# Moving the high and low parts of six early weight conversions from ScalarE and VectorE to GpSimd

## The chip, the cores and the metric

One core of a Trainium2 chip runs the whole program. The metric is the device time of one execution in microseconds (us); several executions of each kernel are timed, and their median is compared. Engines are named as in the profile: PE is TensorE's matrix multiply, PEld its weight loads, ACT is ScalarE, DVE is VectorE, POOL is GpSimd and SP is SyncE, which here only issues DMAs.

## What is computed

The reference chains three blocks in float32: sliding-window attention with a distance bias, a gated block, and a second gated block with one more product inside.

```python
scores = scale * np.matmul(q, k.transpose(0, 1, 3, 2))      # q, k, v: 4 x 8 x 576 x 64
scores = np.where(mask, scores + bias[None], -1000000000.0) # window of 128 keys
attn = softmax(scores); attn_out = np.matmul(attn, v)
x = attn_out.transpose(0, 2, 1, 3).reshape(2304, 512)
x = (x @ w_a) * (x @ w_b) @ w_out                           # d_ff 1536
x = ((x @ w1) * (x @ w2) @ w3) @ w_out2                     # d_ff 1024
```

The weights reach the kernel as 64-bit floats. Each is brought on the core to a float32 value and then divided into a high part (rounded to the type that TensorE multiplies) and a low part, the rest. A product of two such numbers is three matmuls: high by low, low by high, high by high.

## The kernel before

**Stages.** The attention runs in 48 steps: four batches, three runs of query blocks in each (`RUNS`, line 36), four head pairs in each run. A step's scores (line 341, PE) are given their bias and row extremum on DVE (line 368), the exponential on ACT (line 374), and are transposed back (line 406, PE), copied out of PSUM (`pt`, line 273 on ACT or line 275 on DVE) and multiplied with v (line 428, PE). In the first two runs of batch 0 the division by the row sum comes last: PE makes a matrix of reciprocals (line 434), ACT copies it (`r`, line 450), DVE multiplies (`y`, line 452), and POOL makes the high part `x_hi` (line 458) and the low part `x_lo` (line 78, called from line 459). `r` and `y` have one buffer each: the next `y` is written only when POOL has read the last one.

**Filler.** The first gated block's matmuls for group 0 (line 593, `g1`) are put between the steps of the attention as filler. The first tile of 256 tokens is batch 0's first run: it reads `x_hi` and `x_lo` of all four head pairs, its low weights first, then `x_lo` with high weights, then the high parts. Its product is copied by ACT (`a`, line 600), multiplied on DVE (`g`, line 602), and parted into `gh` (ACT, line 605) and `gl` (POOL, line 78).

**The six conversions.** Group 0 has two chunks of weights with three matrices each, six pieces of 128x512, converted beside batch 0's steps. One conversion (`convert`, line 103) is a chain over two engines: ACT takes the absolute value (`ca`, line 113) and the exponent's marker (`ce`, line 116); DVE clamps, shifts and merges (lines 120, 123, 127, 132), all on `ca`; then `split` (line 140) writes the high part `whA` and the low part `wlA`. `ca` has three buffers and `ce` has one. Conversions are named below by the order in which they are made: the first two are the two factors of chunk 0, the third and fourth those of chunk 1, the fifth and sixth the two output matrices. Each engine works its own queue in order; PE's order is written out by hand during the attention (line 819), while that of ACT, DVE and POOL is set at build time by a scheduler, from the times that it expects.

Of the kernel before, what the change touches and what calls it, by code (L numbers as in the profile page):

```python
# [15 lines left out]
ACTF = mybir.ActivationFunctionType  # L16
# [28 lines left out]
def attention_moe_moe(ctx, tc, q, k, v, w_a, w_b, w_o, w_1, w_2, w_3, w_o2, out):  # L45
    nc = tc.nc
# [27 lines left out]
    def f32(ap):  # L74
        return ap.bitcast(F32)

    def sub(eng, out, a, b):
        eng.tensor_tensor(out=out, in0=a, in1=b, op=ALU.subtract)  # L78
# [3 lines left out]
    pools = {}  # L82
# [20 lines left out]
    def convert(raw, hi=None, lo=None, use=()):  # L103
# [32 lines left out]
        if hi is None:  # L136
            return [s0, s1, s3] + [lambda f=f: f(a) for f in use]
        return [s0, s1, s3, lambda: split(a, hi, lo)]

    def split(f, hi, lo):  # L140
        nc.scalar.activation(hi, f, ACTF.Copy)
        sub(nc.vector, lo, f, f32(hi))

    class Stages:

# [93 lines left out]
    raws, v_t = {}, {}  # L239
# [31 lines left out]
    def evict(eng, out, in_):  # L271
        if eng is nc.scalar:
            eng.activation(out, in_, ACTF.Copy)
        else:
            eng.tensor_copy(out=out, in_=in_)

    def prep(run, n):
        b, (x, i) = blocks_of(run)[0], items(run)[n]
        m = rows(i)
        hold = []  # L280

        def trans():
            ps = ps_t.tile([P, W], F32, name="tr")[:, 0:NP * m].rearrange("p (h c) -> p h c", h=NP)
            hold.append(ps)
            t = raws.pop((b, x, i))
            for hp in range(NP):
                nc.tensor.transpose(ps[:, hp, :], t[0:m, hp * P:(hp + 1) * P], ident[0:m, 0:m])  # L287

        def parted():
            ps = hold[0]  # L290
            if x == 0 and m == LAST:
                dst = [(slice(j * D, (j + 1) * D), q_t2, slice(j * D, (j + 1) * D)) for j in range(2)]
            else:
                dst = [(slice(0, P), k_t if x else q_t, slice(i * P, i * P + m))]
            if run < WHOLE:
                nc.scalar.activation(w_t[x][:, :, i * P:(i + 1) * P], ps, ACTF.Copy)
                if x == 0 or i < NB - 2:
                    return
            if b == 0:
                for o, _, c in dst:  # L300
                    d = last_t[x][o, :, (i - NB + 2) * P:][:, :, :m] if x else last_t[x][o, :, c]
                    nc.scalar.activation(d, ps[o], ACTF.Copy)
                return
            for o, (hi, lo), c in dst:
                nc.scalar.activation(hi[o, :, c], ps[o], ACTF.Copy)
                sub(nc.vector, lo[o, :, c], ps[o], f32(hi[o, :, c]))

        return trans, parted
# [216 lines left out]
    def weight_parts(g):  # L525
# [23 lines left out]
        def stages(raw, n, z):  # L549
            hi, lo = [t[:, z].rearrange("p k f -> p (k f)") for t in wt[g, n]]  # L550

            def count():
                whole[g] = whole.get(g, 0) + 1

            if z < 2 or blk == 0:
                return convert(raw, hi, lo) + [count]

            def add():
                nc.vector.tensor_tensor(out=raw[:, 0:W], in0=raw[:, 0:W], in1=raw[:, W:2 * W], op=ALU.add)

            return [add, lambda: split(raw[:, 0:W], hi, lo), count]
# [226 lines left out]
    pools["A", 0] = ctx.enter_context(tc.tile_pool(name="wA0", bufs=1))  # L788
    pools["A", 1] = ctx.enter_context(tc.tile_pool(name="wA1", bufs=1))
    first = ExitStack()  # L790
    pools.update(conv=first.enter_context(tc.tile_pool(name="conv_a", bufs=1)), raws=4, cas=3)
    whole_p = first.enter_context(tc.tile_pool(name="whole_p", bufs=1))
    w_t = [whole_p.tile([P, NP, WHOLE * 2 * P], F32, name=f"w_{x}") for x in "qk"]
    early_p = first.enter_context(tc.tile_pool(name="early_p", bufs=EARLY))
# [13 lines left out]
    for x in range(len(items(1))):  # L808
        load_item(1, x)
        f, g = prep(0, x)  # L810
# [29 lines left out]
    asb.close()  # L840
    acc_half(2)
    conv_b = ctx.enter_context(tc.tile_pool(name="conv_b", bufs=1))
    pools.update(conv=conv_b, raws=2, cas=3)
    pools["B", 0] = pools["B", 1] = ctx.enter_context(tc.tile_pool(name="wB", bufs=1))
    ps_h = ctx.enter_context(tc.tile_pool(name="ps_h", bufs=6, space=PSUM))
    pools["mm"] = [ps_g, ps_h, ps_h, ps_h]
# [38 lines left out]
```

## Time and profile before

| | us |
|---|---|
| median of 3 runs | 951.36 (950.31 to 952.17) |
| the profiled execution, whole | 951.15 |
| its span, first to last instruction | 949.3 |
| PE busy in the span | 935.1 (99%) |
| DVE, ACT, POOL busy | 539.2, 418.6, 168.1 |
| mean granted TensorE clock | 0.997 of full speed |

A row of the timeline gives the start in the span, the duration, engine, line, operation, output and inputs with shapes, how many were merged (x4), and in brackets the idle time of the engine ahead of it with what ended it. Instructions on DVE and ACT overlap a little: the next one starts before the duration of the last is over (0.60 us from start to start for a 128x512 merge that is listed with 0.68). The chain of waits is the work that ended last, followed back from the last instruction.

### The profile page before, as it was taken

The page shows a single profiled execution, that of the slowest core. Times are in us where ns is not written, and L with a number is a line of the kernel's source. Part 1 is how long each engine was busy: PE and PEld are TensorE (multiplying, and loading weights), DVE is VectorE, ACT ScalarE, POOL GpSimd, SP SyncE. Part 2 cuts the span into 40 slices and gives each one's busy share as a digit, 9 for nine tenths or more (in the row PEclk, how much of TensorE's full clock was granted, in tenths as well). Part 3 has the DMA queues.
Part 4 walks back from the last instruction along what each step waited for, and adds up shares of the span by engine and source line. Part 5 has one row for each costly group of instructions (what it writes and reads, how often), then busy time and mean ns, then how long its engine had stood idle before and what let it go on. Part 6 is the DMA issues. An engine that isn't in the chain of part 4 may idle for free.

```text
span 949.3 us, 13998 instructions
## 1 busy us (share of the span) xinstructions
PE 935.1 (99%) x5350; PEld 782.0 (82%) x5350; DVE 539.2 (57%) x1275; ACT 418.6 (44%) x944; POOL 168.1 (18%) x155
## 2 busy tenths in 40 slices
PE   7999999999999999999999999999999999999998
PEld 5788878878888888888888888888888888888886
DVE  4979787828985457575745834813813822522222
ACT  6978777836753345344534522524321421311111
POOL 4210000011212111121111121445211112111111
PEclk9999999999999999999999999999999999999999
DMA  9542423014441223132412310300400400000112
GB/s 232 140 106 57 100 51 64 1 35 144 133 134 56 78 89 123 56 111 95 140 44 81 115 61 25 109 1 1 134 0 1 133 1 1 23 1 1 44 61 95
DMA packets 90371, 68.28 MB, mean 72 GB/s; under 512 B 58304, under 2 KB 79296, under 8 KB 90304
## 3 DMA queue, kind: packets, MB, share of 16 engines
q1 hardware_dynamic: 90304, 67.38, 24.6%
q8 instruction: 42, 0.69, 0.3%
q14 instruction: 25, 0.20, 0.1%
HBM read 58.20 MB, written 8.91 MB: 71 GB/s over the span
## 4 chain that ended last, share of the span: by engine, by line
PE 92%; DVE 4%; ACT 3%; issue 1%; DMA 0%; POOL 0%; DVEq 0%
PE mm L593 51%; PE mm L645 13%; PE mm L661 10%; PE mm L497 5%; PE tr L428 3%; PE s L341 2%; PE mm L621 2%; ACT pe L374 2%; PE tr L406 2%; PE tr L287 2%; DVE pe L368 1%; DVE pe L388 1%; PE mm L489 1%; PE mm L633 1%; DMA early<-in_q 0%
## 5 line engine op out<-in xcount | busy, mean ns | idle before, releaser
L78 POOL TENSOR_TENSOR gl<-g,gh 128x512 fp32r<-128x512 f32 (+1 forms) x102 | 125.3, 1228 | 737.6 <-ACT gh L605 737.6
L602 DVE TENSOR_TENSOR g<-a,mm 128x512 f32<-128x512 f32 (+1 forms) x102 | 63.4, 622 | 202.6 <-PE mm L593 201.5
L605 ACT ACTIVATE gh<-g 128x512 fp32r<-128x512 f32 (+1 forms) x102 | 59.0, 579 | 150.3 <-DVE g L602 149.5
L600 ACT ACTIVATE a<-mm 128x512 f32<-128x512 f32 (+1 forms) x102 | 55.3, 542 | 122.9 <-PE mm L593 122.8
L593 PE MATMUL mm<-x_hi,wlA 128*128 128x512 f32 (+1 forms) x416 | 102.7, 368 | 0.4 <-DVE wlA L78 0.4
L593 PE MATMUL mm<-x_lo,whA 128*128 128x512 f32 (+1 forms) x416 | 99.7, 361 | 0.1
L593 PE MATMUL mm<-x_hi,whA 128*128 128x512 f32 (+1 forms) x416 | 99.4, 361 | 0.0
L593 PE MATMUL mm<-x_lo,whB 128*128 128x512 f32 (+1 forms) x400 | 98.7, 368 | 0.0
L593 PE MATMUL mm<-x_hi,wlB 128*128 128x512 f32 (+1 forms) x400 | 98.6, 368 | 0.0
L593 PE MATMUL mm<-x_hi,whB 128*128 128x512 f32 (+1 forms) x400 | 98.1, 368 | 0.0
L116 ACT ACTIVATE ce<-raw,pad 128x512 int32<-128x512 uint32 x76 | 58.0, 763 | 65.9 <-DVE ca L132 33.3
L593 PEld LDWEIGHTS mm<-x_lo,whA 128*128 128x128 f32 x416 | 72.5, 188 | 12.5 <-POOL x_lo L78 0.3
L593 PEld LDWEIGHTS mm<-x_hi,whA 128*128 128x128 f32 x416 | 72.5, 189 | 12.1
L593 PEld LDWEIGHTS mm<-x_hi,wlA 128*128 128x128 f32 x416 | 71.3, 189 | 13.2 <-issue 1.3
L593 PEld LDWEIGHTS mm<-x_hi,wlB 128*128 128x128 f32 x400 | 71.2, 188 | 12.7
L593 PEld LDWEIGHTS mm<-x_lo,whB 128*128 128x128 f32 x400 | 71.1, 189 | 12.5
L593 PEld LDWEIGHTS mm<-x_hi,whB 128*128 128x128 f32 x400 | 71.0, 189 | 12.5
L649 DVE TENSOR_TENSOR acc<-acc,mm 128x512 f32<-128x512 f32 (+1 forms) x100 | 62.0, 629 | 32.7 <-PE mm L645 32.3
L374 ACT ACTIVATE pe<-pe,st 128x256 f32<-128x256 f32 (+1 forms) x144 | 68.5, 479 | 11.4 <-DVE st L368 10.8
L113 ACT ACTIVATE ca<-raw 128x512 f32<-128x512 f32 x76 | 50.8, 668 | 49.6 <-DMA raw<-in_moe_w 23.6
L132 DVE SCALAR_TENSOR_TENSOR ca<-ce,ca 128x512 int32<-128x512 int32 x76 | 57.3, 754 | 12.2 <-ACT ce L116 10.0
L127 DVE SCALAR_TENSOR_TENSOR ca<-raw,ca 128x512 int32<-128x512 int32 x76 | 61.4, 808 | 1.7
(137 smaller groups left out, 1549.8 us busy)
## 6 DMA issues: line engine op xcount, KB each, us to landing
raw<-in_moe_w SPq DMA_DIRECT2D x32, 512.0 KB, 3.7
raw<-in_moe_w_out SPq DMA_DIRECT2D x20, 512.0 KB, 3.5
raw<-in_moe_w_a SPq DMA_DIRECT2D x12, 512.0 KB, 3.6
raw<-in_moe_w_b SPq DMA_DIRECT2D x12, 512.0 KB, 3.6
out<-acc SPq DMA_DIRECT2D x18, 256.0 KB, 2.0
v<-in_v SPq DMA_DIRECT2D x16, 256.0 KB, 4.0
w<-ce SPq DMA_DIRECT2D x16, 256.0 KB, 2.0
raw<-w SPq DMA_DIRECT2D x16, 256.0 KB, 2.8
```

What stands on the lines that cost most here:

```text
L78: eng.tensor_tensor(out=out, in0=a, in1=b, op=ALU.subtract)
L116: nc.scalar.activation(e, lw, ACTF.Relu, bias=seven, scale=-(2.0 ** -29))
L127: nc.vector.scalar_tensor_tensor(out=ai, in0=hw, scalar=-(1 << 30), in1=ai, op0=ALU.bitwise_and, op1=ALU.bitwise_or)
L132: nc.vector.scalar_tensor_tensor(out=ai, in0=es[0], scalar=7, in1=ai, op0=ALU.bitwise_xor, op1=ALU.bitwise_or)
L374: nc.scalar.activation(pe[:, j, :n], pe[:, j, :n], ACTF.Exp, bias=st[:, 0, j:j + 1], scale=-1.0, accum_out=st[:, 1, j:j + 1],)
L593: nc.tensor.matmul(p, w[:, z, kk, :], x[:, kk], start=(y == 0), stop=(y == len(terms) - 1))
L600: nc.scalar.activation(a, ps[0], ACTF.Copy)
L602: nc.vector.tensor_tensor(out=gg, in0=a, in1=ps[1], op=ALU.mult)
L605: nc.scalar.activation(gh, gg, ACTF.Copy)
L645: nc.tensor.matmul(p, w, x, start=(y == 0), stop=(y == len(terms) - 1))
L649: nc.vector.tensor_tensor(out=ya, in0=ya, in1=p, op=ALU.add)
L661: nc.tensor.matmul(p, x, w, start=(y == 0), stop=(y == len(terms) - 1))
```

## The change

`split` takes its engines from a switch. While the first pool of conversions is open (batch 0), both parts are made by POOL: the high part as a copy with a cast (line 275, `evict`), the low part as a subtraction (line 78). The later conversions keep ACT and DVE; ACT's instruction is the same, only its line is now that of `evict` (273).

```diff
     def split(f, hi, lo):
-        nc.scalar.activation(hi, f, ACTF.Copy)
-        sub(nc.vector, lo, f, f32(hi))
+        evict(nc.gpsimd if pools["beside"] else nc.scalar, hi, f)
+        sub(nc.gpsimd if pools["beside"] else nc.vector, lo, f, f32(hi))
...
-    pools.update(conv=first.enter_context(tc.tile_pool(name="conv_a", bufs=1)), raws=4, cas=3)
+    pools.update(conv=first.enter_context(tc.tile_pool(name="conv_a", bufs=1)), raws=4, cas=3, beside=True)
...
-    pools.update(conv=conv_b, raws=2, cas=3)
+    pools.update(conv=conv_b, raws=2, cas=3, beside=False)
```

The orders of PE and SP stay as they were; from about 60 us on those of ACT, DVE and POOL do too.

On POOL, at the first tile's activations (`ca_251`, `ca_260`, `ca_311`, `ca_376`, `ca_385`, `ca_451` are conversions one to six, `y_605` is the last head pair of run 0), the difference reads:

```order
+L275 CAST whA1_245<-ca_311 128x512
 L458 CAST x_hi_67<-y_605 128x256
+L275 CAST whA1_245<-ca_376 128x512
+L78 TENSOR_TENSOR wlA1_246<-ca_311,whA1_245 128x512
 L78 TENSOR_TENSOR x_lo_68<-y_605,x_hi_67 128x256
+L78 TENSOR_TENSOR wlA1_246<-ca_376,whA1_245 128x512
+L275 CAST whA0_239<-ca_385 128x512
+L275 CAST whA1_245<-ca_451 128x512
+L78 TENSOR_TENSOR wlA0_240<-ca_385,whA0_239 128x512
+L78 TENSOR_TENSOR wlA1_246<-ca_451,whA1_245 128x512
 L78 TENSOR_TENSOR gl_659<-g_656,gh_658 128x256
```

The last `x_lo` of the first tile followed its `x_hi` directly; now the cast of the fourth conversion and the subtraction of the third stand between them.

On ACT, around the first product of the filler (`a_654`, `gh_658`) and the transposed probabilities `pt_682` and `pt_689`, the difference reads:

```order
+L116 ACTIVATE ce_453<-raw_309,pad_73 128x512
 L113 ACTIVATE ca_451<-raw_309 128x512
 L600 ACTIVATE a_654<-mm_629 128x256
+L605 ACTIVATE gh_658<-g_656 128x256
 L273 ACTIVATE pt_682<-tr_677 128x512
 L273 ACTIVATE pt_689<-tr_684 128x512
-L116 ACTIVATE ce_453<-raw_309,pad_73 128x512
-L141 ACTIVATE whA0_239<-ca_385 128x512
-L605 ACTIVATE gh_658<-g_656 128x256
```

The sixth conversion's `ce` moved ahead of `a`, and `gh` moved ahead of the two `pt` copies.

On DVE, behind the fifth conversion, the difference reads:

```order
 L120 TENSOR_SCALAR ca_451<-ca_451 128x512
+L123 TENSOR_SCALAR ca_451<-ca_451 128x512
+L127 SCALAR_TENSOR_TENSOR ca_451<-raw_309,ca_451 128x512
+L132 SCALAR_TENSOR_TENSOR ca_451<-ce_453,ca_451 128x512
 L602 TENSOR_TENSOR g_656<-a_654,mm_629 128x256
```

The product `g` stood behind the first of the sixth conversion's four DVE instructions; now it stands behind all four.

## Rows read from the trace of the kernel before

**Rows 1.** The page: chain that ended last, shares of the span by engine.
```profile
PE 92%; DVE 4%; ACT 3%; issue 1%; DMA 0%; POOL 0%; DVEq 0%
```
**Rows 2.** Chain of waits in order of time: start us, us, what.
```profile
28.22 0.68 DVE wlA L78
...
32.64 0.58 DVE wlA L78
...
38.01 1.67 PE mm L593 x12
...
51.51 1.43 PE mm L621 x12
```
**Rows 3.** Busy time by stretch: PE, PEld, DVE, ACT, POOL, clock, DMA share, GB/s.
```profile
19.00:38.00 19.00, 17.80 (x155) 12.52 (x155) 18.27 (x64) 18.94 (x54) 5.70 (x8) 1.00 0.97 238
```
**Rows 4.** Timeline of DVE, conversions and first products.
```profile
26.06 0.62 DVE L120 TENSOR_SCALAR ca<-ca 128x512 f32<-128x512 f32 x1
...
34.83 1.01 DVE L127 SCALAR_TENSOR_TENSOR ca<-raw,ca 128x512 int32<-128x512 int32 x1
...
36.61 0.65 DVE L132 SCALAR_TENSOR_TENSOR ca<-ce,ca 128x512 int32<-128x512 int32 x1
...
38.32 0.43 DVE L120 TENSOR_SCALAR ca<-ca 128x512 f32<-128x512 f32 x1 [0.46 <-ACT ca L113]
...
39.39 0.69 DVE L127 SCALAR_TENSOR_TENSOR ca<-raw,ca 128x512 int32<-128x512 int32 x1
...
41.73 0.41 DVE L602 TENSOR_TENSOR g<-a,mm 128x256 f32<-128x256 f32 x1
...
44.38 1.22 DVE L78 TENSOR_TENSOR wlA<-ca,whA 128x512 fp32r<-128x512 f32 x1
...
46.13 0.41 DVE L452 TENSOR_TENSOR y<-tr,r 128x256 f32<-128x256 f32 x1
```
**Rows 5.** Timeline of POOL.
```profile
34.55 0.73 POOL L78 TENSOR_TENSOR x_lo<-y,x_hi 128x256 fp32r<-128x256 f32 x1
43.83 1.23 POOL L78 TENSOR_TENSOR gl<-g,gh 128x256 fp32r<-128x256 f32 x1 [8.54 <-ACT gh L605]
...
52.35 0.40 POOL L458 CAST x_hi<-y 128x256 fp32r<-128x256 f32 x1 [1.68 <-DVE y L452]
...
113.25 1.28 POOL L78 TENSOR_TENSOR gl<-g,gh 128x512 fp32r<-128x512 f32 x1 [24.64 <-ACT gh L605]
```
**Rows 6.** Timeline of ACT around the first product.
```profile
40.35 0.69 ACT L113 ACTIVATE ca<-raw 128x512 f32<-128x512 f32 x1
40.92 0.39 ACT L600 ACTIVATE a<-mm 128x256 f32<-128x256 f32 x1
41.19 1.08 ACT L273 ACTIVATE pt<-tr 128x512 f32<-128x512 f32 x2
42.14 0.79 ACT L116 ACTIVATE ce<-raw,pad 128x512 int32<-128x512 uint32 x1
42.81 0.64 ACT L141 ACTIVATE whA<-ca 128x512 fp32r<-128x512 f32 x1
43.33 0.42 ACT L605 ACTIVATE gh<-g 128x256 fp32r<-128x256 f32 x1
```
**Rows 7.** Timeline of PE's weight loads, then of its matmuls, at the first tile.
```profile
35.34 0.19 PEld L593 LDWEIGHTS mm<-x_lo,whA 128*128 128x128 f32 x1 [0.28 <-POOL x_lo L78]
...
38.01 0.71 PE L593 MATMUL mm<-x_hi,wlA 128*128 128x256 f32 x4 [0.38 <-DVE wlA L78]
...
47.41 0.66 PE L287 MATMUL tr<-ident,raw 128*128 128x128 f32 x4
```
**Rows 8.** PE after its longest wait behind DVE, and two stretches after it.
```profile
127.01 1.23 PE L406 MATMUL tr<-ident,pe 128*128 128x128 f32 x8 [1.71 <-DVE pe L388]
...
128.00:130.00 2.00, 2.00 (x16) 1.61 (x16) 1.97 (x10) 1.08 (x3) 0.00 (x0) 0.55 0.00 0
130.00:132.00 2.00, 2.00 (x15) 1.58 (x14) 1.63 (x9) 0.66 (x3) 0.00 (x0) 0.59 0.01 2
```

## Prediction, made before the changed kernel ran

> **What bounds the kernel now.** I read the page first: PE is on 92% of the chain that ended last, POOL on 0% [rows 1]. So work moved to POOL is free only where POOL's result isn't waited for, and work taken from DVE or ACT pays only where the chain runs over them. The chain in order of time shows where that is: DVE's pieces lead up to 38 us, two low-part subtractions at 28.22 and 32.64 among them, and from 38.01 on PE's matmuls take over [rows 2]. The table by stretch says the same: from 19 to 38 us DVE is busy 18.27 of 19.00 us, ACT 18.94, POOL 5.70 [rows 3]. This is the stretch that the change aims at, and POOL looks idle in it. The timelines then show who waits for whom: PE's load for the last `x_lo` of the first tile waits for POOL at 35.34, and the first matmul of chunk 1 for DVE's `wlA` at 38.01 [rows 7]. POOL is on no chain, but it already feeds the place where the chain passes from DVE to PE.
>
> **The two engines block each other.** DVE's merge at 34.83 took 1.01 us, the same instruction at 39.39 took 0.69 [rows 4]; POOL's `x_lo` ran from 34.55 to 35.28 [rows 5], and the merge ended 0.56 us after that: it did its work when POOL was done. At 44.38 the subtraction took 1.22 us, and ended 0.54 us behind POOL's `gl` (43.83 + 1.23 = 45.06) [rows 4, 5]. That `gl` has itself 0.50 us more than the 0.73 of the same shape, since it came while a merge ran. So an instruction of DVE with two SBUF inputs (lines 127, 132, 78) and one of POOL exclude each other, and take turns. Line 120, with one input, took 0.62 at 26.06 and 0.43 at 38.32 [rows 4]: it is in this too.
>
> **The change part by part.**
>
> *Removed from ACT:* six casts, listed like the one at 42.81 with 0.64 us [rows 6]. ACT is full from 19 to 38 [rows 3] but the chain there is DVE's; I count 0. If DVE weren't late, ACT would be next.
>
> *Removed from DVE:* six subtractions. Two lie ahead of the fourth conversion's last merge (36.61) and on the chain: 0.6 + 0.6 = 1.2 us [rows 2, 4]. The other four come behind it; what they would give is under the second path.
>
> *Added to POOL:* six subtractions of 128x512, 1.28 us each [rows 5], and six casts of that size, which no row shows. The 128x256 cast takes 0.40 [rows 5]; twice the size lies between 0.40 and 0.80. Going from 256 to 512 the subtraction grows from 0.73 to 1.28, by 1.75; I take nearly the same growth off a smaller fixed part and get 0.62. In all 6 x 1.28 + 6 x 0.62 = 11.4 us more on POOL. [...]
>
> *Blocking up to 37 us.* Ahead of the fourth merge POOL gets three casts and two subtractions, 3 x 0.62 + 2 x 1.28 = 4.4 us, in which DVE's conversion instructions are blocked. Between 0 (they never meet) and 4.4 us, I take 0.9: the two stalls above, 0.19 and 0.33, came with 5.70 us of POOL's work [rows 3], which would make 0.4 of 4.4, but POOL's new instructions are longer and start right behind a merge, with another one of the same kind behind it. Against the relief of 1.2 the fourth merge then starts at 36.3 in place of 36.61, and is done at 36.9.
>
> *First path, POOL's order.* The last `x_lo` now stands behind the fourth conversion's cast, which waits for that merge, and behind the third conversion's subtraction. With 0.1 between instructions (an estimate; 52.35 and 113.25 show durations alone) and one turn of DVE (0.43, line 120 at 38.32): 36.9 + 0.1 + 0.62 + 0.1 + 1.28 + 0.43 + 0.1 + 0.73 = 40.3, against 34.55 + 0.73 = 35.28 [rows 5]: 5.0 us late. PE then has 17 matmuls of the tile left, 0.12 each (12 of that width took 1.43 at 51.51 [rows 2]), so chunk 1 starts at 40.3 + 0.1 + 2.0 = 42.4 in place of 38.01 [rows 7]: **+4.4 us**. The wait of 0.38 on `wlA` is gone in that. PE's order is fixed, so everything stands behind this wait, the attention's transposes too.
>
> *Second path, DVE and ACT.* The fifth conversion's first three DVE instructions meet POOL's train (the subtraction, `x_lo`, the next subtraction) one by one. Its merge of line 127 starts after that train, 40.3 + 0.43 + 1.28 = 42.0, in place of 39.39, and the last merge ends at 42.0 + 0.69 + 0.1 + 0.65 = 43.4 [rows 4, 5]. `ce` has one buffer, so the sixth conversion's line 116 waits until then on ACT, with line 113 and `a` behind it: 43.5 + 0.67 + 0.57 (from the starts at 42.14, 42.81 and 40.35, 40.92) = 44.7, not 40.92 [rows 6]. `g` now stands behind the sixth conversion's four instructions: 44.7 + 0.1 + 0.43 + 0.43 + 0.69 + 0.65 = 47.0, not 41.73 [rows 4]. `gh` follows at 47.4, not 43.33, and the `pt` copies behind it at 47.7, not 41.19 [rows 6]. From those copies to `y` it was 46.13 - 41.19 = 4.9 us, in which ACT had 1.6 us (42.14 to 43.33 + 0.42 = 43.75 [rows 6]) of `ce`, the cast and `gh`, which stand there no longer: `y` at 47.7 + 4.9 - 1.6 = 51.0. PE's transposes at 47.41 need the PSUM that `y` reads: 51.0 + 0.4 = 51.4, **+4.0 us**. `y` has one buffer, so later ones wait for POOL too.
>
> *The sum.* Both paths arrive at nearly the same lateness, and since they run side by side only the longer counts: 4.4 us. Beyond 51.5 us the chain is PE's again [rows 2], nothing there gives time back, and what POOL still has to do for the fifth and sixth weights (two casts and two subtractions, 3.8 us behind the sixth conversion's last merge at 47.0) is done by 51, ahead of line 621, which needs them at 51.51 + 4.4. The later conversions change by 0. The profiled execution took 951.15 (span 949.3 and 1.85 around it), 0.2 below the median; 951.36 + 4.4 = **955.8**.
>
> **The rivals.**
>
> [...]
>
> *The queue hardly binds.* If POOL and DVE met as seldom as before, the fourth merge would end near 36.1 and `x_lo`, with no turn of DVE between, at 36.1 + 0.1 + 0.62 + 0.1 + 1.28 + 0.1 + 0.73 = 39.0, chunk 1 at 41.1, 3.1 us late. But then `y`, with five subtractions fewer ahead of it on DVE, comes before PE's transposes at 47.41 ask for it, and what PE now waits there is given back. That lies between 0 and +3.1; I take +0.5, near the low end, since `y` is the later of the two today: 951.9.
>
> *Faster.* The end is set by `y` at 46.13, through PE's transposes at 47.41. DVE loses five subtractions ahead of it, 4 x 0.6 and the blocked one's 1.1 = 3.5 us. If the first tile's `x_lo` came by 36 us, PE would gain the 0.38 at 38.01 and between 0 and 3.5 at 47.41; the middle is 2.1: 951.4 - 2.1 = 949.3. It needs a fourth merge 3 us earlier than I find; against it is the order on POOL, which is fixed.
>
> **How the numbers follow.** Chances: forecast 0.60, with the clock 0.16, hardly binding 0.16, faster 0.08. A measurement here can tell 0.2%, 1.9 us. Range: at the low end the case that hardly binds (951.9, and 0.3 for the spread of runs), at the high end casts of 0.80 (five in a row on the path, +0.9), the clock (+1.7) and 0.3: 951.6 to 958.6. Slower by over 0.2%: 0.60 + 0.16 = 0.76; within: 0.16; faster: 0.08.
>
> **What would show it.** Right: POOL's last `x_lo` of the first tile ends near 40, its casts last near 0.62; DVE's conversion rows between 24 and 43 of over 0.9 us become many; PE's wait ahead of that tile names POOL, chunk 1 starts at 42 or later; `y` of the first pair of run 1 near 51; from 52 us on everything shifted by the same amount. Wrong: chunk 1 before 40, or a shift that shrinks between 50 and 100 us, or DVE's rows unblocked beside POOL's.

## The result

| | us |
|---|---|
| before, median of 6 runs | 950.86 (950.00 to 952.33) |
| after, median of 6 runs | 955.59 (954.77 to 956.63) |
| ratio after to before | 1.0051, 95% interval 1.0040 to 1.0061 |
| the profiled execution after, whole | 956.29 |
| its span | 954.5 |

The change costs 4.7 us, 0.5%. The six executions after it lie in two groups, 954.77 to 955.03 and 956.14 to 956.63, the second with a lower mean granted clock (0.996 for 0.997 and 0.998); the profiled one is of the second group. In the span PE is busy 937.2 us (935.1 before), DVE 538.4, ACT 416.1 and POOL 179.3. The page of the changed kernel gives the chain that ended last, by engine (before: [rows 1]):

```profile
PE 91%; DVE 4%; ACT 3%; POOL 1%; issue 1%; DMA 0%; DVEq 0%
```

POOL has come onto the chain. The table by stretch of the changed kernel, with the columns of [rows 3] and [rows 8], shows where:

```profile
19.00:38.00 19.00, 16.41 (x140) 10.71 (x137) 18.33 (x61) 17.41 (x49) 10.54 (x14) 1.00 1.01 244
...
38.00:51.00 13.00, 11.36 (x91) 10.45 (x91) 8.77 (x25) 8.21 (x25) 7.40 (x8) 0.87 0.04 7
51.00:64.00 13.00, 13.00 (x141) 11.15 (x140) 8.55 (x30) 9.03 (x25) 5.21 (x9) 1.00 0.49 104
...
40.00:42.00 2.00, 2.00 (x13) 2.00 (x11) 1.97 (x3) 0.50 (x3) 1.00 (x1) 0.53 0.00 0
42.00:44.00 2.00, 2.00 (x13) 2.00 (x13) 0.82 (x4) 1.18 (x2) 0.61 (x1) 0.62 0.00 0
...
132.00:134.00 2.00, 1.89 (x10) 1.50 (x10) 1.76 (x9) 1.80 (x7) 0.00 (x0) 0.57 0.47 103
134.00:136.00 2.00, 2.00 (x20) 1.78 (x22) 1.71 (x8) 0.60 (x1) 0.00 (x0) 0.58 0.00 0
```

From 38 to 51 us in the kernel before:

```profile
38.00:51.00 13.00, 12.96 (x137) 11.18 (x138) 11.79 (x35) 12.68 (x36) 4.37 (x6) 1.00 0.17 39
```

From 19 to 38 us DVE stays as busy as in [rows 3] (18.33 for 18.27 us) although three subtractions left it (61 instructions for 64): blocked time counts as busy, as in the 1.78 us of line 127 at 25.30, 0.69 where nothing disturbs it [rows 4]. PE lost 1.39 us there, and from 38 to 51 it worked 11.36 us where it had worked 12.96; from 40 to 44 its granted clock was 0.53 and 0.62 of full speed, with 0.50 in every part from 40.4 to 43.2, (0.47 + 0.38) x 2 = 1.7 us lost. From 51 us on PE is full again. The half clock at 132 to 136 is the one of [rows 8], 5 us later.

The timeline of POOL in the changed kernel (before: [rows 5]):

```profile
36.30 0.80 POOL L458 CAST x_hi<-y 128x256 fp32r<-128x256 f32 x1 [1.23 <-DVE y L452]
37.04 0.61 POOL L275 CAST whA<-ca 128x512 fp32r<-128x512 f32 x1
37.62 1.28 POOL L78 TENSOR_TENSOR wlA<-ca,whA 128x512 fp32r<-128x512 f32 x1
38.85 0.73 POOL L78 TENSOR_TENSOR x_lo<-y,x_hi 128x256 fp32r<-128x256 f32 x1
39.54 1.46 POOL L78 TENSOR_TENSOR wlA<-ca,whA 128x512 fp32r<-128x512 f32 x1
```

The last `x_lo` of the first tile ends at 39.58, 4.3 us later than in [rows 5], behind a cast and a subtraction. The timeline of PE (before: [rows 7]):

```profile
32.12 0.66 PE L428 MATMUL tr<-pt,v 128*64 128x128 f32 x8 [1.07 <-ACT pt L273]
...
37.15 0.39 PE L593 MATMUL mm<-x_hi,wlA 128*128 128x256 f32 x1 [0.80 <-POOL x_hi L458]
...
39.64 0.39 PE L593 MATMUL mm<-x_lo,whA 128*128 128x256 f32 x1 [1.75 <-POOL x_lo L78]
...
40.51 1.06 PE L593 MATMUL mm<-x_hi,wlA 128*128 128x256 f32 x4
...
43.06 0.84 PE L593 MATMUL mm<-x_hi,wlA 128*128 128x256 f32 x4
...
52.59 0.66 PE L287 MATMUL tr<-ident,raw 128*128 128x128 f32 x4
...
56.36 0.48 PE L621 MATMUL mm<-gh,wlA 128*128 128x256 f32 x2
```

Line 621 in the kernel before:

```profile
51.27 0.48 PE L621 MATMUL mm<-gh,wlA 128*128 128x256 f32 x2
```

Two waits name POOL, then four matmuls take 1.06 us where they take 0.64 at full clock (44.22 in the same timeline). Chunk 1 starts at 43.06 for 38.01, the transposes of 47.41 come at 52.59, and line 621 at 56.36 for 51.27: 5.1 us, and between 43 and 56 no wait. The timeline of DVE (before: [rows 4]) and that of ACT (before: [rows 6]):

```profile
25.30 1.78 DVE L127 SCALAR_TENSOR_TENSOR ca<-raw,ca 128x512 int32<-128x512 int32 x1
...
31.61 1.30 DVE L120 TENSOR_SCALAR ca<-ca 128x512 f32<-128x512 f32 x1
...
36.15 0.68 DVE L132 SCALAR_TENSOR_TENSOR ca<-ce,ca 128x512 int32<-128x512 int32 x1
36.75 0.42 DVE L368 CUSTOM_DVE_ANT_0 pe<-s,relb 128x256 f32<-128x256 f32 x1
...
38.89 0.97 DVE L120 TENSOR_SCALAR ca<-ca 128x512 f32<-128x512 f32 x1 [0.68 <-ACT ca L113]
39.90 1.39 DVE L123 TENSOR_SCALAR ca<-ca 128x512 int32<-128x512 int32 x1
41.32 0.69 DVE L127 SCALAR_TENSOR_TENSOR ca<-raw,ca 128x512 int32<-128x512 int32 x1
...
46.45 0.41 DVE L602 TENSOR_TENSOR g<-a,mm 128x256 f32<-128x256 f32 x1
...
50.61 0.43 DVE L452 TENSOR_TENSOR y<-tr,r 128x256 f32<-128x256 f32 x1
```

```profile
42.82 0.78 ACT L116 ACTIVATE ce<-raw,pad 128x512 int32<-128x512 uint32 x1 [2.32 <-issue]
...
44.06 0.37 ACT L600 ACTIVATE a<-mm 128x256 f32<-128x256 f32 x1
...
46.90 0.42 ACT L605 ACTIVATE gh<-g 128x256 fp32r<-128x256 f32 x1 [2.46 <-DVE g L602]
47.22 1.06 ACT L273 ACTIVATE pt<-tr 128x512 f32<-128x512 f32 x2
```

The fifth conversion's lines 120 and 123, 0.43 us each when free, take 0.97 and 1.39 beside POOL's train; ACT stands still for 2.32 us ahead of the sixth `ce` and 2.46 ahead of `gh`. This is the second path, and it is nearly as late as the first: `y` at 50.61 for 46.13, 4.5 us. In this execution PE comes to the places that need a `y` later still, and doesn't wait for one.

### The profile page after: what moved, and what is told of

Read it like the earlier page. It is cut to its first block, busy times and chain, and to the rows that moved or that the text cites. A ratio compares the mean times of both kernels' runs of the same rounds, so it can differ in the third digit from the quotient of the medians.

```text
span 954.5 us, 13998 instructions
## 1 busy us (share of the span) xinstructions
PE 937.2 (98%) x5350; PEld 784.6 (82%) x5350; DVE 538.4 (56%) x1269; ACT 416.1 (44%) x938; POOL 179.3 (19%) x167
## 4 chain that ended last, share of the span: by engine, by line
PE 91%; DVE 4%; ACT 3%; POOL 1%; issue 1%; DMA 0%; DVEq 0%
PE mm L593 51%; PE mm L645 13%; PE mm L661 10%; PE mm L497 5%; PE tr L428 3%; PE s L341 2%; PE mm L621 2%; ACT pe L374 2%; PE tr L406 2%; PE tr L287 2%; DVE pe L368 1%; DVE pe L388 1%; PE mm L489 1%; PE mm L633 1%; DVE ca L127 0%
```

## The experiments

Theory A: POOL's order makes the last `x_lo` late, and PE with it. Theory B: the blocked fifth conversion, the single `ce`, `g` and the late `y` hold PE. Theory C: the fallen clock adds to A. Rival D: any conversion work on POOL costs, wherever it lies. Each run is timed against the kernel before; its median was 951.32 in the first two sets and 950.86 in the third.

**Two conversions at a time.** The switch is replaced by the conversion's number.

```diff
-        evict(nc.gpsimd if pools["beside"] else nc.scalar, hi, f)
-        sub(nc.gpsimd if pools["beside"] else nc.vector, lo, f, f32(hi))
+        on = (nc.gpsimd, nc.gpsimd) if next(nth) in (1, 2) else (nc.scalar, nc.vector)
+        evict(on[0], hi, f), sub(on[1], lo, f, f32(hi))
```

Conversions 1 and 2: 

> Only conversions 1 and 2 are split on GpSimd; 3 to 6 as before. Theory A (GpSimd's queue in front of the last x_lo of the first tile is what costs): nothing of these two conversions stands directly ahead of that x_lo, so its end comes back from 39.58 to under 37 us, chunk 1 starts between 38.0 and 40.0 us (before 38.01, changed kernel 43.06), time 951 to 952.5. Theory B (the fifth conversion, ce and the late gate product decide): its stages are back on ScalarE and VectorE, so before's time, 951. Rival D (it is the blocking of VectorE by GpSimd's work, wherever it falls): a third of the loss stays, 952.5 and more.

Measured 951.66, ratio 1.0006 (0.9998 to 1.0015). The last `x_lo` ends at 37.50, where A wanted under 37, and chunk 1 starts at 39.69, 1.7 us late. PE's timeline, at line 621:

```profile
52.80 0.48 PE L621 MATMUL mm<-gh,wlA 128*128 128x256 f32 x2
```

That is 1.5 us late, and line 633 near 223 us is still 1.5 us late (224.99 for 223.48), so the delay is not taken up later. The medians are only 0.3 us apart, but more executions of this run kept the full clock, five of 11 against five of 24: those with a mean clock of 1.000 took 950.77 to 951.60 here and 949.84 to 950.12 in the kernel before, 1.0 us apart in their middle. So these two conversions cost something although nothing of them stands directly ahead of that `x_lo`. B, which had before's time, doesn't hold, and D isn't refuted by this run.

Conversions 3 and 4, with `(3, 4)` in that line: 

> Only conversions 3 and 4 are split on GpSimd. Theory A: the cast of conversion 4 and the subtractions of 3 and 4 still stand round the last x_lo; chunk 1 starts 2.5 to 4 us later than before (40.5 to 42), time 953.5 to 955.5, with the half clock after the wait in the upper part. Theory B: the fifth conversion is as before; at most 1 us is lost, 951 to 952.

Measured 953.67, ratio 1.0030 (1.0019 to 1.0042). PE's timeline:

```profile
37.39 0.39 PE L593 MATMUL mm<-x_lo,whA 128*128 128x256 f32 x1 [1.64 <-POOL x_lo L78]
...
51.69 0.66 PE L428 MATMUL tr<-pt,v 128*64 128x128 f32 x8 [0.64 <-DVE y L452]
```

A's time, but in this trace only in part by A's way: chunk 1 is late by 1.5 us (39.53), not 2.5 to 4, and PE then waits again, for `y`. The traced execution is the fastest of six, 951.79 at full clock, 1.9 us over the kernel before at full clock; the others took 953.09 to 955.21 with lower clocks, and where chunk 1 starts in them isn't shown. Part runs have a limit that shows here: the scheduler puts another order on POOL, the fourth conversion's cast now behind the last `x_lo`.

Conversions 5 and 6, with `(5, 6)`: 

> Only conversions 5 and 6 are split on GpSimd. Theory A: they stand behind the last x_lo in GpSimd's order; chunk 1 starts as before (38.0, within 0.5 us), time 951 to 951.5. Theory B: the fifth conversion is blocked and late, so g and the first y of the second run come late, PE waits for y or pt between 45 and 52 us; time 953 to 955.

Measured 951.32, ratio 1.0003 (0.9994 to 1.0011); chunk 1 at 37.83, no wait for `y`. B in the form that this expectation gave it, the fifth conversion blocked by its own parts on POOL, falls, and so does D: the work of these two conversions is on POOL and costs nothing that can be told, where D would have a third of the loss, 1.6 us. The three parts add to 2.7 us by the medians and to about as much by the executions at full clock (1.0, 1.9 by a single one, and none); the whole is 4.7: they don't simply add.

**PE kept busy in the two waits.** Matmuls of zeros go into the open accumulation ahead of the last `x_hi` (`y == 3`) and the last `x_lo` (`y == 7`) of the first tile.

```diff
+                for _ in range({3: 7, 7: 14}.get(y, 0) if (g, n, t, z) == (0, 0, 0, 0) else 0):
+                    nc.tensor.matmul(p, warm[:, 0:P], warm[:, 0:tn], start=False, stop=False)
```

> The changed kernel with 7 and 14 matmuls of zeros (fp16, 256 columns) added to PE's order where it waits for the last x_hi and the last x_lo of the first tile; they add zeros to an open accumulation and so change no value. Theory C (the wait costs its own length and then a clock at half speed for 3.4 us): the granted clock stays at 1.00 between 39 and 44 us, chunk 1 starts at 41.3 to 41.9 (43.06 without them), time 953.6 to 954.4. Without C: the clock falls all the same or its fall cost nothing, 955.6.

Measured 955.53, ratio 1.0048 (1.0036 to 1.0061). PE's timeline:

```profile
39.08 0.39 PE L595 MATMUL mm<-x_lo,whA 128*128 128x256 f32 x1 [0.20 <-POOL x_lo L78]
...
53.19 0.66 PE L428 MATMUL tr<-pt,v 128*64 128x128 f32 x8 [0.65 <-DVE y L452]
```

The clock stayed at 1.00 from 38 to 44 us and chunk 1 started at 41.22, about as C said, but the time did not follow. PE ran into the second path: 0.65 us of waiting for the `y` of run 1's second pair. So B lives on in another form: what blocks the fifth conversion is POOL's work for the third and fourth.

**One part of each conversion.** The high parts alone on POOL (`sub(nc.vector, lo, f, f32(hi))` as before): 

> Only the high parts are made on GpSimd, in all six conversions; the low parts stay on VectorE. Theory A (GpSimd's queue in front of the last x_hi and x_lo of the first tile): between them stands one cast of 0.61 us instead of casts and subtractions of 3.2 us; PE waits under 1 us for that x_lo, chunk 1 starts at 38.3 to 40, time 951 to 952.5. Theory B (the first y of the second run comes late because VectorE's conversion operations are blocked): no long subtraction runs on GpSimd, little blocking, PE doesn't wait for y, 951 to 952. Rival D (any conversion work on GpSimd costs): half of the loss, 953 and more.

Measured 952.38, ratio 1.0008 (0.9999 to 1.0017): no wait for `x_lo`, and a wait of 0.71 for `y`. The low parts alone (`evict(nc.scalar, hi, f)`): 

> Only the low parts are made on GpSimd, in all six; the high parts stay on ScalarE. Theory A: the subtractions of conversions 3 and 4 (1.28 us each) stand round the last x_lo as in the changed kernel; chunk 1 starts at 40.5 to 42.5, time 953 to 955.5. Theory B: the fifth conversion is blocked by the same subtractions, PE waits for y near 52; time 953 to 955.5 too. If instead the casts were what costs: 951.5 or less.

Measured 955.73, ratio 1.0046 (1.0034 to 1.0059), as much as the whole change. DVE's timeline there:

```profile
36.88 1.64 DVE L132 SCALAR_TENSOR_TENSOR ca<-ce,ca 128x512 int32<-128x512 int32 x1
...
40.68 1.82 DVE L132 SCALAR_TENSOR_TENSOR ca<-ce,ca 128x512 int32<-128x512 int32 x1
```

Merges that take 0.65 [rows 4] stood behind subtractions of 1.27 and 1.28 us on POOL (36.70 and 40.67). PE waited 2.02 us for `x_hi`, which came late since DVE's `y` did, and 1.14 for `x_lo`, and its clock was down from 37 to 43 us (0.66, 0.50, 0.50 and 0.63 in the four stretches of 2 us from 36 on), twice as long as in the changed kernel; the one execution with a mean clock of 0.998 (the others have 0.995 and 0.996) took 953.85, so a part of this loss may be the clock's. The casts alone cost 1.1 us, with an interval that just reaches none; the subtractions alone bring the loss back, in POOL's queue and on DVE.

**`x_lo` out of POOL's queue.** Line 459 becomes `sub(nc.vector, lo, ps, f32(hi))`. 

> The changed kernel, but the x_lo of batch 0 are made on VectorE, out of GpSimd's queue. Theory A alone: PE waits for the last x_hi (0.8 us as now) and not for x_lo on GpSimd; chunk 1 starts at 39.5 to 41, time 952.5 to 954. Theory B close behind A, as the run with PE kept busy showed (PE waited for y at 53.2 there): chunk 1 comes early, but PE then waits for y of the first pair of run 1 between 49 and 53 us, and most of the loss stays, 953.5 to 955.5.

Measured 956.14, ratio 1.0057 (1.0043 to 1.0070), nothing won. The traced execution is the fastest of five (954.23; the others took 956.13 to 957.85). PE's timeline:

```profile
38.48 0.58 PE L593 MATMUL mm<-x_lo,whA 128*128 128x256 f32 x1 [2.00 <-DVE x_lo L78]
```

The wait went over to DVE, whose merge ahead of that `x_lo` took 1.03 us beside POOL. So it isn't POOL's order alone: in DVE's queue, behind a blocked merge, `x_lo` comes late too. No run took the first path away and left the second.

**The clock at the late places.** The kernel before, with zeros where its clock was seen to fall: at 127 us [rows 8], and, in runs above, at 204 to 214, where PE waits 0.42 us for `gh` and 0.62 for `gl` (0.57 from 206 to 210 in the run with conversions 1 and 2).

```diff
+        for _ in range(15 if (step, i) == ((2, 1, 0), 2) else 0):
+            nc.tensor.matmul(ps[:, 0:2 * P], warm[:, 0:P], warm[:, 0:2 * P], start=True, stop=True)
...
+                for _ in range({1: 4, 3: 5}.get(y, 0) if (t, m) == (1280, 0) else 0):
+                    nc.tensor.matmul(ps[:, x, 0:2 * P], warm[:, 0:P], warm[:, 0:2 * P], start=False, stop=False)
```

> The kernel before, with matmuls of zeros in PE's order at the two places where its clock was seen to fall after a wait: 15 of them ahead of the transposes that wait 1.71 us at 127 us, and 4 and 5 in the product that waits 0.42 and 0.62 us for gh and gl at 204 to 206 us. Theory C (the waits let the clock fall, about 1.5 us each time, in some executions): granted clock 1.00 in every stretch, times between 949.8 and 950.5 in nearly all executions, 0.1% under the kernel before's median. Otherwise the median stays at 951.3, or rises by what the added matmuls take beyond the waits.

Measured 949.96 (949.36 to 950.48), ratio 0.9989 (0.9980 to 0.9998): faster than both kernels, as C said. Table by stretch, then PE's timeline (line numbers are now 2 or 4 higher):

```profile
128.00:130.00 2.00, 2.00 (x27) 1.70 (x27) 1.97 (x9) 1.31 (x3) 0.00 (x0) 1.00 0.00 0
```

```profile
126.01 1.80 PE L404 MATMUL tr<-warm 128*128 128x256 f16 x15 [0.86 <-DVE x_lo L78]
127.64 1.04 PE L408 MATMUL tr<-ident,pe 128*128 128x128 f32 x8
```

The clock is 1.00 where it was 0.55 [rows 8]. The zeros waited 0.86 us for DVE's `x_lo`, which reads PSUM, and the transposes came at 127.64 for 127.01: fewer than 15 may do better, which wasn't tried.

**The change without clock noise.** The changed kernel with these late zeros, so that only the clock at 40 us is left: 

> The changed kernel with the added matmuls of zeros of the faster version at its two late places (127 and 204 us in the kernel before), so that only the clock at 40 us can still differ. Its distance to that version (949.96) is what the change costs up to 56 us. Theory A with C: 4.1 to 5.1, the half clock at 40 us included; time 954.1 to 955.1, with two groups of executions about 1 us apart if the clock falls in only some of them.

Measured 955.38, ratio 1.0047 (1.0035 to 1.0060), above the range that was expected. Its base, 949.96, is of the second set; in this set the executions of the kernel before with a mean clock of 1.000 took 950.07 to 950.38, in their middle 950.22, and the loss against that is 5.2. With the 7 and 14 early zeros too: 

> The same with the 7 and 14 matmuls of zeros at the waits for the last x_hi and x_lo as well: granted clock 1.00 everywhere. Theory A alone at full clock would give 3.2 to 3.7 more than 949.96, 953.2 to 953.7; theory B as the next bound (PE waits for y of run 1's first pair, as in the run with the early fill alone) gives 4.1, 954.1, and then the clock at 40 us costs nothing of its own: time as with two fills, within 0.5.

Measured 954.96, ratio 1.0046 (1.0033 to 1.0058), 4.7 over 950.22 and more than the 4.1 that B had. Table by stretch and PE's timeline of the last:

```profile
40.00:42.00 2.00, 2.00 (x19) 2.00 (x19) 1.97 (x4) 0.13 (x2) 0.63 (x1) 1.00 0.00 0
```

```profile
41.38 0.64 PE L597 MATMUL mm<-x_hi,wlA 128*128 128x256 f32 x4
...
53.33 0.66 PE L430 MATMUL tr<-pt,v 128*64 128x128 f32 x8 [0.65 <-DVE y L454]
...
55.20 0.48 PE L625 MATMUL mm<-gh,wlA 128*128 128x256 f32 x2
```

The same places in the kernel before with late zeros:

```profile
37.86 0.71 PE L595 MATMUL mm<-x_hi,wlA 128*128 128x256 f32 x4 [0.38 <-DVE wlA L78]
...
51.09 0.48 PE L625 MATMUL mm<-gh,wlA 128*128 128x256 f32 x2
```

Against these, chunk 1 is 3.5 us late and line 625 is 4.1 late; the wait for `y` lies between. At the transposes near 77 us it is 4.6 with the early zeros, where PE waits 0.87 us for `pe` (0.40 in the other two), and 4.9 without. So of the 1.7 us that PE loses at half clock 0.3 reach 77 us; the medians differ by 0.4, which their intervals don't tell from none.

**Which conversions, once more.** Conversions 1 to 4 on POOL: 

> Conversions 1 to 4 on GpSimd, 5 and 6 as before, with the two late fills. Theory A: everything that stands round the last x_lo is there, chunk 1 as late as in the changed kernel, 953.5 to 955. Theory B (the fifth conversion's train decides): 1 us or less over 949.96. If the parts simply add (0.3 and 2.4 us were measured for conversions 1, 2 and 3, 4): 952.7.

Measured 956.28, ratio 1.0058 (1.0045 to 1.0070), more than the whole change with the same late zeros in the same set (955.38). Table by stretch and PE's timeline:

```profile
38.00:40.00 2.00, 1.11 (x9) 1.11 (x10) 1.81 (x2) 1.75 (x6) 2.00 (x3) 1.00 0.03 7
40.00:42.00 2.00, 2.00 (x19) 2.00 (x19) 1.97 (x5) 0.00 (x0) 0.27 (x1) 1.00 0.00 0
```

```profile
36.40 0.39 PE L595 MATMUL mm<-x_hi,wlA 128*128 128x256 f32 x1 [0.81 <-POOL x_hi L460]
...
38.89 0.38 PE L595 MATMUL mm<-x_lo,whA 128*128 128x256 f32 x1 [1.75 <-POOL x_lo L78]
...
52.31 0.66 PE L287 MATMUL tr<-ident,raw 128*128 128x128 f32 x4 [0.69 <-DVE y L454]
...
54.92 0.66 PE L430 MATMUL tr<-pt,v 128*64 128x128 f32 x8 [0.65 <-DVE y L454]
```

POOL's order up to the last `x_lo` is that of the changed kernel, and so are PE's two waits. The clock didn't fall there in the traced execution (the fastest of five), chunk 1 started at 41.02, earlier than in the changed kernel, and the end is later: PE waits for `y` twice (and 0.97 for `pt` at 49.07), because ACT and DVE now have the casts and subtractions of conversions 5 and 6 to do ahead of `g` (47.67 for 46.45). The second path decides here. A foresaw 955 at most, B 1 us at most in its first form; neither had it that conversions 5 and 6 are better off on POOL once 1 to 4 are there.

Conversions 3 to 6: 

> Conversions 3 to 6 on GpSimd, 1 and 2 as before, with the two late fills. If the parts add (2.4 and 0.0): 952.3. If the late end of conversions 1 and 2, which is 0.3 us alone, pushes 3 and 4 together in the changed kernel: the loss here stays under that with conversions 1 to 4, 951.8 to 953. Theory B: 953.5 to 954.5.

Measured 952.90, ratio 1.0019 (1.0010 to 1.0028), 2.7 over 950.22. Taking conversions 1 and 2 off POOL saves 2.5 of the 5.2 us that the changed kernel with late zeros loses, though alone they cost 1.0 at full clock. They make PE wait 1.07 us for `pt` (32.12 in the changed kernel; not in this run). How much of the 2.5 is theirs stays open: here too the cast of conversion 4 stands behind the last `x_lo`.

## Why the prediction held, and where it didn't

The forecast was 955.8, the measurement 955.59; the loss 4.4, measured 4.7. That the number fits so well is in part luck, as two of the steps show:

- **The blocking.** DVE and POOL took turns as forecast, for longer than forecast. Line 127 at 25.30 took 1.78 us beside a subtraction of POOL that ran from 25.26 to 26.53, and ended 0.55 behind it, like the rows that the step was read from. The fourth merge was put at 36.3 and came at 36.15, but by two errors that cancel: from 20 us up to that merge DVE's instructions took about 2.0 us longer from start to start than before (1.2 of them on line 127, 0.9 on line 120, as at 31.61), where the sum has 0.9; and four score instructions of line 368, 1.4 us, that ran ahead of the merge from 34.14 on now run behind it (36.75), which the sum doesn't have.
- **The casts.** Right: 0.62 forecast, 0.61 where nothing disturbs them (37.04), 0.74 to 0.81 beside DVE's work. The subtractions were put at 1.28 and took 1.27 to 1.28, once 1.46. From 256 to 512 columns the cast grew by 0.21 us (0.40 [rows 5] to 0.61); the fixed part is 0.40 - 0.21, about 0.19 us, by my estimate.
- **First path.** The mechanism is right, the size too large. `x_lo` was to end at 40.3 and ended at 39.58: the turn of DVE (0.43) that I put into POOL's train didn't come, and POOL's instructions start 0.58 and 1.23 us apart, less than the durations plus 0.1. The train began at 37.04 as forecast, but behind `x_hi`, whose `y` came late (35.83 for 33.47), and not behind the merge; PE's wait of 0.80 for that `x_hi` is not in the forecast. At full clock chunk 1 is 3.5 us late, not 4.4.
- **Second path.** Right nearly row by row: line 127 of the fifth conversion 42.0 forecast and 41.32 measured, `a` 44.7 and 44.06, `g` 47.0 and 46.45, `pt` 47.7 and 47.22, `y` 51.0 and 50.61. It was put at +4.0, and at full clock line 625 is 4.1 late. Only the place is one step off: with the early zeros the transposes of 47.41 come just as the first pair's `y` has ended (50.72, `y` 50.23 + 0.42), and PE waits for the second pair's. Its links weren't parted by a run: a second buffer for `ce` wasn't tried.
- **The sum.** The step that failed is that the first path is the longer. At full clock the second one is, by about 0.6 us at 55 us; PE's wait for `y` stands in the runs with early zeros. In the traced execution of the changed kernel the first path is the longer, but only with the half clock. The term of 4.4 was 0.9 too large; that the second path lies close behind, and that only the longer counts, is what made the number right.
- **The shift from 52 us on.** 5.1 us at lines 593, 287 and 621, and 5.0 at line 633 near 223: constant within 0.2, as said. In the full-clock pair it grows from 4.1 to 4.6 by the longer wait for `pe`.
- **The rival with the clock.** The 1.7 us that the range has for it are what PE lost at 0.55 and 0.59 of its clock in [rows 8], (0.45 + 0.41) x 2; no run shows them as a loss of time. In the traced execution the clock did fall, by those 1.7 us of PE's work, and it hardly cost anything, since the second path covers that time: in the two runs with late zeros, without and with the early ones, 0.3 of it reach 77 us and the medians are 0.4 apart. Waits alone don't settle whether it falls: behind waits of 0.80 and 1.75 us it was 0.53 at 40 us in the changed kernel, and behind the same two waits 1.00 in the run with conversions 1 to 4. What settles it wasn't shown.
- **The other rivals.** That the queue hardly binds is refuted by the two waits on POOL. The gain would have needed `x_lo` by 36 us. Both of these rivals also take it that PE waits for `y` at 47.41 in the kernel before; that row has no wait in brackets [rows 7], and PE was busy 12.96 of the 13.00 us from 38 to 51, so there was nothing to win or to give back there.

## What to carry to other kernels

An engine with idle time is no free place for work if its results feed the critical engine through an in-order queue (the last `x_lo` ended 4.3 us later behind a cast and a subtraction), or if its work blocks the engine that was to be relieved (line 127 took 1.78 us for 0.69): count what stands behind each moved instruction on its new queue. Where two paths to the same end are late by nearly the same amount, work out both; taking one away (here the slow clock) then returns almost nothing. Where the clock falls in some executions only, compare executions with the same clock: by the medians conversions 1 and 2 cost 0.3 us, at full clock 1.0. A wait of PE may cost more than its length (the zeros at the late places won 1.4 us), and a few matmuls of zeros in that wait are a cheap way to see what its clock is worth.

## What the runs showed that was not expected

*The clock falls in some executions only.* The first set's 24 executions of the kernel before had mean granted clocks from 0.996 to 1.000, and times from 949.84 to 952.54 us; the five at 1.000 took 949.84 to 950.12. In the traces, up to the last matmul, it fell at one or two of three places (36 to 44, 128 to 136, 204 to 214 us), behind waits of PE of 0.42 to 2.02 us where its timeline was read, and in some traces at none. With zeros at the two late places all 11 executions lay at 0.999 or 1.000, between 949.36 and 950.48.

*Which work of DVE is blocked doesn't go by size.* With conversions 3 and 4 on POOL a row of four columns took 1.26 us, 0.16 where nothing disturbs it, beside a subtraction of POOL (39.59 to 40.94); DVE's timeline:

```profile
39.72 1.26 DVE L381 TENSOR_SCALAR st<-st 128x4 f32<-128x4 f32 x1
```

That row ended 0.04 us behind POOL's subtraction. DVE's instructions of 128x256 with an input in PSUM (lines 368, 452, 602) kept 0.39 to 0.43 us beside POOL's work in the changed kernel. Why the one is blocked and the others are not wasn't shown.
